# First to second expert layer: the last two units routed as one group, the exit beside the first matmul group, weight splits moved into the head's second matmuls

## The chip, the cores and the metric

The kernel runs on one core of a Trainium2 chip. The metric is the device time of one execution in microseconds; before the change the median of three runs is 629.38 us (629.02 to 632.44). Engines are TensorE (PE, with its weight loads shown as PEld), VectorE (DVE), ScalarE (ACT), GpSimd (POOL) and SyncE (SP, which here issues DMAs). Each works through its own queue in the order in which the program was written.

## What is computed

Attention over clusters, then two mixture-of-experts layers one behind the other. Both layers pick one expert of eight for each of 1536 rows of 512 numbers, multiply by two weight matrices with a ReLU between them, and scale by the gate. The second layer's routing needs the first layer's result, row by row.

```python
def _moe2_ref(x, w_gate, w_output_gate, w1, w2) -> np.ndarray:
    logits = x @ w_gate
    e_idx = np.argmax(logits, axis=1)
    ...
    eom = 1.0 / (1.0 + np.exp(-(x @ w_output_gate)))
    out = np.zeros((N, D), dtype=np.float32)
    for e in range(E):
        mask = e_idx == e
        ...
        h = np.maximum(x[mask] @ w1[e], 0.0)
        ye = h @ w2[e]
        out[mask] = gate_w[mask, None] * eom[mask, e, None] * ye
    return out.astype(np.float32)
...
    x = _moe_ref(x=x, **moe_kwargs)
    return _moe2_ref(x=x, **moe2_kwargs)
```

## The kernel before

Attention takes about the first 300 us; the change is in the two expert layers behind it. They are cut into 18 units, 0 to 8 for the first layer and 9 to 17 for the second. A unit is the rows of one expert (the largest expert of each layer is two units: 0 and 1, 9 and 10), in tiles of at most 128 rows: unit 6 has 128 and 48 rows, unit 7 128 and 40, unit 8 has 120, unit 9 two of 128, unit 10 128 and 8, unit 11 128, 128 and 16. The first unit of a layer is its head.

`run` (L1050) writes out the order of all work by hand. A unit has eight groups of first matmuls, f=0 to f=7 (`mm1`, L916: 12 matmuls each, then `hh` on ACT and the rest `hl` on DVE), and four quarters of second matmuls, d=0 to d=3 (`mm2`, L976; unit 9 takes `mm2_by_token`, L952, in which ACT copies each quarter out into `xo` and sums it into `ls`, a tile that `outs` (L936) has POOL set to zero at d=0). Ahead of each f and d, `run` takes as many steps of the open background tasks as `SB` says for a head (one for other units), and as many weight splits as the unit's row of `PIECES` says. A split is a half of one weight chunk of 1 MB: `wh` on ACT and, one split later, the rest `wl` on DVE (L820, L827); when a chunk is split its buffer is free and `pump` (L795) has SP load a next one into it (`raw`).

Background tasks are the exits. `exit1` (L1620) of a unit of the first layer is put on the list behind group `fx` of the next unit: f=7 for most, f=2 (`FB`) where the next unit is the second layer's head. Its steps: logits `pq` from the unit's result `y`, and `lt` on ACT; `pg` and the transposes `pyo` back; then `lg` on DVE, and the rows `xo` on ACT, tile by tile. The copy of the last quarter of `y` is on DVE, that of the others on ACT (L998). Units are routed in groups (`group1`): the last unit of a group goes on into `routed` (L1670): choice of the expert, counts `cs`, gate, scales `sx` and the scaling of `xo` on POOL (L1711), the places by two matmuls `ppos` (L1718, L1719), the gate's copy into the row on POOL (L1755), the write to the table `x2d` in DRAM from SP (L1760), and the inverse list by one-hot tiles `av`, `rv` and a matmul (L600). Group (4, 5) also picks the second layer's first expert and gives the list `idx2a` for unit 9. The last group has all rows in place: it gives `idx2` for the units from 10 on and issues the gathers of units 10 and 11.

A `gather` (L857) is an indirect DMA for each tile from POOL, out of `x2d` into `xg`; `meta` (L873) reads two columns of it on POOL; `entry` (L891) transposes a tile on PE (`pxt`), copies it on ACT (`xh`) and takes the rest on DVE (`xl`). For most units the entry of the next unit's tiles stands behind f=4 to f=7; in a head it stands behind d=3. A unit's gather is issued by `run` ahead of f=0 where it isn't out yet, as for unit 9, behind the steps that are due there.

In `routed`, `last` is the group with unit 8: it takes its choice at once, and has two steps of pause (`KL`) between its one-hot tiles and the inverse matmul.

Of the kernel before, what the change touches and what calls it, by code (L numbers as in the profile page):

```python
# [473 lines left out]
def turns_by(k, *chains):  # L474

    chains = list(chains)
    while chains:
        for _ in range(k):
            chains = [c for c in chains if next(c, c) is not c]
        if chains:  # L480
            yield
# [195 lines left out]
class Stage:  # L677


    def __init__(self, units, src, w1, w2, sw):  # L680
        self.src, self.w, self.sw = src, (w1, w2), sw
        self.units = [Unit(self, *u) for u in units]
        n = r = 0
        for i, u in enumerate(self.units):
            u.first, u.row = n, r
            n += len(u.tiles)
            r += u.rows
            u.closes = i + 1 == len(units) or self.units[i + 1].j != u.j
            u.opens = i == 0 or self.units[i - 1].j != u.j
        self.ranks = list(dict.fromkeys(u.j for u in self.units))  # L690
        self.E = len(self.ranks)
        self.reg = [None] * self.E
        self.exit = None


class Unit:
    def __init__(self, stage, j, tiles):
        self.stage, self.j, self.tiles, self.rows = stage, j, tiles, sum(tiles)
        self.idx = None
        self.src = stage.src  # L700
        self.gt = None
        self.by_token = False
        self.last = False
        self.xo = None


class MoE:
# [23 lines left out]
    FX = 1  # L731
    FB = 2
    FY = 7
    SA = (1, 0, 1, 0, 1, 1, 0, 1, 1, 0, 1, 1)
    SB = (1, 3, 2, 1, 1, 1, 1, 1, 1, 1, 1, 1)
    Q = 2

    def __init__(self, tc, ctx, ident, R, XW, ND, stages, ps_t):
# [237 lines left out]
    def mm2(self, u, d):  # L976
        nc = self.nc
        if u.by_token:
            return self.mm2_by_token(u, d)
        N = u.rows  # L980
        if d == 0:
            u.y = self.y.tile([128, 4, self.most], F32, tag="yt", name="yt", bufs=1)
        hh, hl = u.h
        self.need(4 * u.r + 2 + d // 2)
        wh, wl = (w.rearrange("p (a f) -> p a f", a=8) for w in self.chunk[4 * u.r + 2 + d // 2])
        p = self.ps_mm.tile([128, 512], F32, tag="m", name="py")
        s = slice(d % 2 * 128, d % 2 * 128 + 128)
        k = 0
        for (w, x) in ((wh, hh), (wl, hh), (wh, hl)):
            if u.last and k == 16:  # L990
                if d == 0:
                    self.outs(u)
                else:
                    self.turn(u, d - 1)
            for f in range(8):
                nc.tensor.matmul(p[:, :N], w[:, f, s], x[:, f, :N], start=(k == 0), stop=(k == 23))  # L996
                k += 1
        (nc.vector.tensor_copy if d == 3 else nc.scalar.copy)(u.y[:, d, :N], p[:, :N])  # L998
        if u.last and d == 3:
            self.turn(u, d)  # L1000

# [48 lines left out]
    def run(self, task):  # L1050

        units = self.units
        self.tasks.append(task)
        for i, u in enumerate(units):
            prev = units[i - 1] if i else None
            nxt = units[i + 1] if i + 1 < len(units) else None
            head = not prev or prev.stage is not u.stage
            steps = (1,) * 12 if not head else self.SB if prev else self.SA
            fx = self.FB if head else self.FX if not nxt else self.FY if nxt.stage is not u.stage else 7
            own = 4 * u.r + 8 if head else self.G  # L1060
            pieces = self.PIECES[i]
            for f in range(8):
                for _ in range(steps[f]):
                    self.step()
                if not head and self.ngather == i + 1:
                    self.gather()
                if not head and self.nmeta == i + 1 < self.ngather:
                    self.meta()
                self.pieces(pieces[f], own)
                self.mm1(u, f)  # L1070
                if f == 3 and u.closes:
                    self.limit += 1
                if prev and f == fx:
                    self.exit(prev)
                if f >= 4 and nxt and not head:
                    self.entry(nxt, f - 4)
            if u.closes:
                self.limit += 1
            for d in range(4):
                for _ in range(steps[8 + d]):  # L1080
                    self.step()
                self.pieces(pieces[8 + d], own)
                if d == 3 and u.opens:
                    self.need(4 * u.r + 3)
                    self.flags(u.r)
                self.mm2(u, d)
                if d % 2 and u.closes:
                    self.limit += 1
                if d == 1 and self.ngather == i + 2:
                    self.gather()  # L1090
                if d == 3 and self.nmeta == i + 2:
                    self.meta()
            if head:
                assert nxt.gt, "unit not gathered"
                for k in range(len(nxt.tiles)):
                    self.entry(nxt, k)
        self.exit(units[-1])
        self.step(all=True)
# [4 lines left out]
KL = 2  # L1103
# [172 lines left out]

def tile_kernel(tc, q, k, v, centroids, wg1, w11, w12, cap_in, wg2, wog2, w21, w22, out,
                prof1=(192, 304, 208, 200, 192, 176, 168, 120), prof2=(392, 272, 224, 192, 160, 128, 120, 88),
                head1=128, head2=256, cut2=5, by_token=(0, 3, 5), group1=((0, 1), (2, 3), (4, 5), (6, 7), (8,)), seq1=(1, 2, 3, 4, 5, 6, 7), seq2=(1, 6, 2, 5, 3, 4, 7), dbg=None):
    nc = tc.nc  # L1280
    P = 128
    B, NP, _, S = q.shape
# [10 lines left out]
    with ExitStack() as ctx:  # L1293
# [326 lines left out]
        def exit1(unit, ys):  # L1620

            group = of[id(unit)]
            ns, gs, u = unit.tiles, unit.gt, unit.u
# [10 lines left out]
            N = unit.rows  # L1634
# [12 lines left out]
            xo = [M.xo.tile([P, XW], F32, tag="xo", name="xo") for _ in ns]  # L1647
            xos += zip(xo, ns)
            ps = back(ys)
            yield  # L1650
            nc.gpsimd.tensor_copy(vb[:, k0:k1], unit.vb)
            nc.gpsimd.tensor_scalar(vk[:, k0:k1], unit.vb, M.okr[unit.r], None, op0=ALU.mult)
            for i, n in enumerate(ns):
# [16 lines left out]
        def routed(group, t0, T, rows):  # L1670
            lg, am, vb, vk, xos = held.pop(id(group))
            last = s1.units[-1] in group
# [19 lines left out]
            K = KC if cut else KG  # L1692
# [19 lines left out]

            if not last:
                yield from turns_by(K[1], scales())
            for _ in range(1 if last else K[5]):
                yield
            pp = M.ps_g.tile([P, 512], F32, tag="g", name="ppos2")
            nc.tensor.matmul(pp[:, :T * E], R.to[:, 0], oh2[:, t].rearrange("p a e -> p (a e)"), start=True, stop=False)  # L1718
# [1 line left out]
            if last or cut:  # L1720
                nc.tensor.matmul(pp[:, T * E:(T + 1) * E], R.to[:, 1], cs2[:, t0 + T], start=True, stop=True)
            lohi, ro = [], []
            yield

            def places():
                nc.vector.tensor_tensor(pos, pp[:, :T * E].rearrange("p (a e) -> p a e", e=E),
# [44 lines left out]
                if not last and K[4]:  # L1771
                    yield
            more = first_experts() if cut else iter(())
            for _ in range(KL if last else K[3]):
                yield
                for _ in range(2):
                    next(more, None)
# [124 lines left out]
```

## Time and profile before

| | us |
|---|---|
| median of three runs | 629.38 |
| lowest, highest | 629.02, 632.44 |
| profiled execution, its own time | 627.58 |
| its span, first to last instruction | 625.7 |
| PE busy in the span | 569.5 (91%) |
| DVE, ACT, POOL busy | 467.1, 419.9, 212.8 |

The profile is of one execution. Time in its views is counted in us from the start of the span. The passage between the layers lies between 437 (unit 8 starts), 455.5 (unit 9), 481.8 (unit 9's last matmul) and 488.5 (unit 10's first). PE's granted clock is given as a share of 2.4 GHz: 1.00 is that level, 0.50 the level of 1.2 GHz. An instruction's idle time stands in brackets behind it, with what ended it.

### The profile page before, as it was taken

To read this page: it belongs to the slowest core of one execution; us is meant where nothing else is said; L and a number is where in the kernel's file an instruction comes from. 1 tells how busy PE (TensorE), PEld (TensorE's weight loads), DVE (VectorE), ACT (ScalarE), POOL (GpSimd) and SP (SyncE) were. 2 spreads that over 40 slices of the span, in tenths; PEclk is the share of its full clock that TensorE was granted. 3 is DMA by queue.
4 is the path that set the end of the run, shared out by engine and by line. 5 is a ranking of instruction groups with operands and counts; after the bars stand their busy time and mean duration, and the time that the engine had idled before them with its cause. 6 is when DMAs were issued, how large, how long until landed. Compare 5 with 4: busy or idle time off the path is not lost.

```text
span 625.7 us, 14519 instructions
## 1 busy us (share of the span) xinstructions
PE 569.5 (91%) x5430; PEld 470.8 (75%) x5430; DVE 467.1 (75%) x1219; ACT 419.9 (67%) x885; POOL 212.8 (34%) x420
## 2 busy tenths in 40 slices
PE   6899999998999988958999998998788899999992
PEld 2766767675767666637878997997767888999992
DVE  5767777679899677756597689788776566989881
ACT  4766666776666669832676776876654466979781
POOL 8702020204150210134615268344333623253341
PEclk9899999999999999998899999999899799999998
DMA  5779391826429952314486776977754457998930
GB/s 148 212 231 275 97 216 46 210 60 151 141 89 233 252 171 82 133 56 138 130 269 204 243 244 179 304 238 244 248 181 152 164 174 238 305 308 298 321 111 20
DMA packets 75518, 117.55 MB, mean 188 GB/s; under 512 B 10504, under 2 KB 43400, under 8 KB 75441
## 3 DMA queue, kind: packets, MB, share of 16 engines
q1 hardware_dynamic: 71585, 105.96, 56.1%
q0 software_dynamic: 3264, 9.72, 4.9%
q8 instruction: 45, 0.74, 0.5%
q10 hardware_dynamic: 592, 0.87, 0.4%
q14 instruction: 32, 0.26, 0.1%
HBM read 84.28 MB, written 12.87 MB: 155 GB/s over the span
## 4 chain that ended last, share of the span: by engine, by line
PE 63%; DVE 16%; ACT 9%; DMA 5%; issue 4%; SPq 1%; POOL 0%; ACTq 0%; DVEq 0%; POOLq 0%
PE ph L930 17%; PE py L996 13%; PE av L280 9%; PE pss L238 7%; PE ppt L268 6%; DVE wl L827 3%; DVE nm L246 3%; PE pz L971 3%; ACT pe L254 2%; PE pyo L1609 2%; PE pxt L907 2%; ACT pt L270 1%; ACT wh L820 1%; DMA xg<-x2d,idx2a 1%; DMA xg<-x2d,idx 1%
## 5 line engine op out<-in xcount | busy, mean ns | idle before, releaser
L827 DVE SCALAR_TENSOR_TENSOR wl<-raw,sw,wh 128x1024 f16<-128x1024 f32 x128 | 163.5, 1283 | 18.5 <-ACT wh L820 18.4
L820 ACT ACTIVATE wh<-raw,sw 128x1024 f16<-128x1024 f32 x128 | 145.7, 1146 | 2.6 <-DMA x<-ot 2.5
L246 DVE TENSOR_REDUCE nm<-pss 128x1 f32<-128x768 f32 x96 | 91.4, 952 | 40.5 <-PE pss L238 36.8
L254 ACT ACTIVATE pe<-pss,nm 128x768 f32<-128x768 f32 x96 | 87.1, 907 | 24.2 <-DVE nm L246 24.2
L930 PEld LDWEIGHTS <-wh 128*128 128x128 f16 x1152 | 91.3, 102 | 14.2 <-issue 9.7
L238 PE MATMUL pss<-y,x 128*128 128x384 f32 x384 | 93.5, 364 | 4.1 <-ACT pe L254 3.2
L268 PE MATMUL ppt<-ident,pe 128*128 128x128 f32 x576 | 80.5, 275 | 3.3 <-ACT pt L270 1.4
L238 PEld LDWEIGHTS pss<-y,x 128*128 128x128 f32 x384 | 63.0, 190 | 24.4 <-issue 12.3
L270 ACT COPY pt<-ppt 128x384 f32<-128x384 f32 x128 | 57.9, 482 | 28.6 <-PE ppt L268 28.2
L268 PEld LDWEIGHTS ppt<-ident,pe 128*128 128x128 f32 x576 | 69.3, 142 | 8.9 <-ACT pt L270 2.3
L930 PE MATMUL ph<-xh,wh 128*128 128x192 f16 (+14 forms) x576 | 69.5, 246 | 6.7 <-DVE hl L933 5.7
L996 PEld LDWEIGHTS <-wh 128*128 128x128 f16 x960 | 72.4, 99 | 3.8 <-issue 0.5
L930 PE MATMUL ph<-xl,wh 128*128 128x192 f16 (+14 forms) x576 | 69.5, 246 | 0.2
L930 PE MATMUL ph<-xh,wl 128*128 128x192 f16 (+14 forms) x576 | 69.5, 246 | 0.0
L280 PE MATMUL av<-pt,v 128*64 128x384 f32 x384 | 68.8, 494 | 0.0
L932 ACT ACTIVATE hh<-ph 128x128 f16<-128x128 f32 (+14 forms) x144 | 44.1, 312 | 35.7 <-PE ph L930 34.3
L933 DVE SCALAR_TENSOR_TENSOR hl<-ph,hh 128x128 f16<-128x128 f32 (+14 forms) x144 | 46.4, 333 | 24.6 <-ACT hh L932 24.0
L930 PEld LDWEIGHTS <-wl 128*128 128x128 f16 x576 | 47.4, 102 | 1.9
L996 PE MATMUL py<-hl,wh 128*128 128x192 f16 (+13 forms) x480 | 46.6, 239 | 0.8 <-DVE hl L933 0.8
L996 PE MATMUL py<-hh,wh 128*128 128x192 f16 (+13 forms) x480 | 46.5, 239 | 0.6 <-DVE hl L933 0.4
L280 PEld LDWEIGHTS av<-pt,v 128*64 128x64 f32 x384 | 24.8, 136 | 28.4 <-issue 28.2
L996 PE MATMUL py<-hh,wl 128*128 128x192 f16 (+13 forms) x480 | 46.1, 239 | 0.0
(319 smaller groups left out, 858.8 us busy)
## 6 DMA issues: line engine op xcount, KB each, us to landing
raw<-in_moe_w SPq DMA_DIRECT2D x64, 1024.0 KB, 5.9
y<-kh SPq DMA_DIRECT2D x31, 192.0 KB, 4.0
x<-qh SPq DMA_DIRECT2D x30, 192.0 KB, 4.2
q<-in_q SPq DMA_DIRECT2D x8, 384.0 KB, 5.1
k<-in_k SPq DMA_DIRECT2D x8, 384.0 KB, 5.3
x<-ql SPq DMA_DIRECT2D x16, 192.0 KB, 3.6
v<-in_v SPq DMA_DIRECT2D x8, 384.0 KB, 4.1
out<-zt SPq DMA_DIRECT2D x1, 3072.0 KB, 11.0
```

The source lines that it names most:

```text
L238: nc.tensor.matmul(p[:, hf, :W], xx[:, c * P:(c + 1) * P], yy[:, hf * W:(hf + 1) * W], start=a, stop=o)
L246: nc.vector.tensor_reduce(nm, p[:, :, :W], axis=AX.XY, op=ALU.max, negate=True)
L254: nc.scalar.activation(pe, p[:, :, :W], AF.Exp, bias=d["nm", c, j], scale=1.0, accum_out=d["sm"][:, c, j:j + 1])
L268: nc.tensor.transpose(p[:, kc * P:(kc + 1) * P], pe[:, kh, kc * P:(kc + 1) * P], ident)
L270: eng(pt[:, kh * HALF:(kh + 1) * HALF, (c % HALF) * P:(c % HALF + 1) * P], p.rearrange("p (a b) -> p a b", a=HALF))
L280: nc.tensor.matmul(p[j * D:(j + 1) * D, :W], d["v"][:, j, kc, :], d["pt", hf, j][:, kc, :], start=(kc == 0), stop=(kc == C - 1))
L820: nc.scalar.activation(hi[:, :, s], x[:, :, s], AF.Copy, scale=sw)
L827: nc.vector.scalar_tensor_tensor(lo[:, :, s], x[:, :, s], sw, hi[:, :, s], op0=ALU.mult, op1=ALU.subtract, accum_out=fl)
L930: nc.tensor.matmul(p[:, :N], w[:, c, fs], x[:, c, :N], start=(k == 0), stop=(k == 11))
L932: nc.scalar.activation(hh[:, f, :N], p[:, :N], AF.Relu)
L933: nc.vector.scalar_tensor_tensor(hl[:, f, :N], p[:, :N], 0.0, hh[:, f, :N], op0=ALU.max, op1=ALU.subtract)
L996: nc.tensor.matmul(p[:, :N], w[:, f, s], x[:, f, :N], start=(k == 0), stop=(k == 23))
```

## The change

- `group1` becomes (0,1), (2,3), (4,5), (6), (7,8): unit 6 is routed alone, the last two units of the first layer as one group of three tiles.
- `FB` 2 to 0: unit 8's exit goes on the list behind f=0 of unit 9, not f=2; `SB` becomes ones. Unit 8's exit leaves out one pause (behind `pyo`), the last group has one pause more ahead of `ppos`, none behind it, and one more ahead of the inverse matmul.
- Unit 8's copy of the last quarter of `y` moves from DVE to ACT.
- `PIECES` of unit 9: splits at f=7 and d=0 to d=3, in place of f=1, f=7, d=1, d=3; unit 10 loses the one at f=0.
- Unit 10's entry: tile 0 ahead of d=2 of unit 9, tile 1 ahead of d=3, in place of both behind d=3.
- The gathers behind d=1 run one unit further ahead in the second layer.

```diff
@@ MoE @@
-              (0, 1, 0, 0, 0, 0, 0, 1, 0, 1, 0, 1),
-              (1, 0, 0, 0, 1, 0, 0, 0, 0, 1, 0, 1),
+              (0, 0, 0, 0, 0, 0, 0, 1, 1, 1, 1, 1),
+              (0, 0, 0, 0, 1, 0, 0, 0, 0, 1, 0, 1),
...
-    FB = 2
+    FB = 0
...
-    SB = (1, 3, 2, 1, 1, 1, 1, 1, 1, 1, 1, 1)
+    SB = (1, 1, 1, 1, 1, 1, 1, 1, 1, 1, 1, 1)
...
-        (nc.vector.tensor_copy if d == 3 else nc.scalar.copy)(u.y[:, d, :N], p[:, :N])
+        (nc.vector.tensor_copy if d == 3 and (u.last or not u.ends) else nc.scalar.copy)(u.y[:, d, :N], p[:, :N])
...
+                if head and prev and d >= 2:
+                    for k in range(d - 2, len(nxt.tiles), 2):
+                        self.entry(nxt, k)
                 self.mm2(u, d)
                 if d % 2 and u.closes:
                     self.limit += 1
-                if d == 1 and self.ngather == i + 2:
-                    self.gather()
+                if d == 1 and not head:
+
+                    for _ in range(i + 3 + (u.stage is not units[0].stage) - self.ngather):
+                        self.gather()
                 if d == 3 and self.nmeta == i + 2:
                     self.meta()
-            if head:
+            if head and not prev:
...
-group1=((0, 1), (2, 3), (4, 5), (6, 7), (8,))
+group1=((0, 1), (2, 3), (4, 5), (6,), (7, 8))
@@ exit1, routed @@
             ps = back(ys)
-            yield
+            if not unit.ends:
+                yield
...
-            for _ in range(1 if last else K[5]):
+            for _ in range(2 if last else K[5]):
                 yield
...
             lohi, ro = [], []
-            yield
+            if not last:
+                yield
...
-            for _ in range(KL if last else K[3]):
+            for _ in range(KL + 1 if last else K[3]):
```

(`ends` is true for the last unit of a layer, `last` for the last unit of all.)

## Rows read from the trace of the kernel before

**Rows 1.** Waits of PE from 290 to 626: total us, times, longest us.
```profile
PE pxt L907 <- DMA xg<-x2d,idx: 4.6, 1, 4.6
...
PE pxt L907 <- DMA xg<-x2d,idx2a: 2.0, 1, 2.0
PE ppos L600 <- DVE rv L595: 1.9, 1, 1.9
...
PE ppos L1719 <- DVE cs L1699: 1.0, 1, 1.0
```

**Rows 2.** Busy us by stretch: length, PE, PEld, DVE, ACT, POOL; PEclk, DMA share, GB/s.
```profile
437.34:455.52 18.18, 14.99 (x223) 13.75 (x220) 14.18 (x41) 13.35 (x27) 6.57 (x13) 0.91 0.77 261
455.52:471.28 15.76, 12.72 (x125) 10.72 (x122) 12.28 (x56) 9.02 (x23) 5.75 (x14) 1.00 0.43 143
471.28:481.80 10.52, 10.52 (x99) 9.27 (x96) 8.72 (x42) 4.32 (x10) 3.28 (x5) 1.00 0.40 127
481.80:488.45 6.65, 1.79 (x10) 1.32 (x9) 0.14 (x1) 1.32 (x5) 5.27 (x14) 0.85 0.80 281
488.45:493.30 4.85, 4.76 (x42) 4.59 (x42) 2.46 (x7) 1.85 (x4) 4.07 (x11) 0.50 0.01 3
```

**Rows 3.** Timeline of PE: start us, us, instruction, idle before and its end.
```profile
445.07 0.71 PE L907 MATMUL pxt<-ident,xg 128*128 128x128 f32 x4 [2.04 <-DMA xg<-x2d,idx2a]
...
486.54 1.64 PE L907 MATMUL pxt<-ident,xg 128*128 128x128 f32 x8 [4.59 <-DMA xg<-x2d,idx]
```

**Rows 4.** Timeline of POOL, 418 to 438: a scaling of group (4, 5), unit 9's gathers.
```profile
418.24 3.91 POOL L1711 TENSOR_SCALAR xo<-xo,sx 128x512 f32<-128x512 f32 x4 [0.82 <-DVE sx L671]
...
435.94 1.11 POOL L867 DMA_INDIRECT xg<-x2d,idx2a  x1 [2.92 <-PE py L996]
437.35 1.48 POOL L867 DMA_INDIRECT xg<-x2d,idx2a  x1 [0.30 <-PE py L996]
```

**Rows 5.** Timeline of DVE: routing steps, a rest of the split, the copy of y.
```profile
416.57 0.75 DVE L1699 TENSOR_TENSOR cs<-cs,oh 128x8 f16<-128x8 f16 x4
...
437.95 0.32 DVE L998 COPY yt<-py 128x168 f32<-128x168 f32 x1
...
472.21 0.42 DVE L933 SCALAR_TENSOR_TENSOR hl<-ph,hh 128x256 f16<-128x256 f32 x1
472.54 0.15 DVE L1726 TENSOR_TENSOR pos<-ppos,base 128x8 f32<-128x8 f32 x1
...
475.44 1.27 DVE L827 SCALAR_TENSOR_TENSOR wl<-raw,sw,wh 128x1024 f16<-128x1024 f32 x1
...
477.21 0.18 DVE L649 TENSOR_REDUCE idx<-w 128x4 int32<-128x32 f32 x1
```

**Rows 6.** Timeline of POOL, 474 to 487: scaling of group (8), first and last gather.
```profile
474.36 0.70 POOL L1711 TENSOR_SCALAR xo<-xo,sx 120x512 f32<-120x512 f32 x1
...
479.21 2.10 POOL L867 DMA_INDIRECT xg<-x2d,idx  x1 [3.99 <-DVE p2nov L663]
...
485.52 0.92 POOL L867 DMA_INDIRECT xg<-x2d,idx  x1 [0.30 <-issue]
```

**Rows 7.** Timeline of ACT: unit 8's last split, unit 9's first copy out.
```profile
457.33 1.14 ACT L820 ACTIVATE wh<-raw,sw 128x1024 f16<-128x1024 f32 x1
...
475.25 0.47 ACT L973 ACTIVATE xo<-pz,u 128x256 f32<-128x256 f32 x1 [3.31 <-POOL ls L939]
```

**Rows 8.** Chain that ended last, around unit 8's small matmuls: start us, us, work.
```profile
463.26 0.34 PE pq L1637 x8
...
463.91 1.33 PE ph L930 x12
...
466.13 3.93 PE ph L930 x36
```

**Rows 9.** DMA issues at 485.5 (gather) and 464.5 (write): KB, us to landing.
```profile
xg<-x2d,idx POOLq DMA_INDIRECT x1, 2.9
...
x2d<-xo SPq DMA_DIRECT2D x1, 262.0 KB, 2.1
```

More of the change, by code (lines that the diff above doesn't have):

```diff
@@ L689, in __init__ @@
             u.opens = i == 0 or self.units[i - 1].j != u.j
+            u.ends = i + 1 == len(units)
         self.ranks = list(dict.fromkeys(u.j for u in self.units))
@@ L703, in __init__ @@
         self.last = False
+        self.ends = False
         self.xo = None
@@ L1278, in tile_kernel @@
                 prof1=(192, 304, 208, 200, 192, 176, 168, 120), prof2=(392, 272, 224, 192, 160, 128, 120, 88),
-                head1=128, head2=256, cut2=5, by_token=(0, 3, 5), group1=((0, 1), (2, 3), (4, 5), (6, 7), (8,)), seq1=(1, 2, 3, 4, 5, 6, 7), seq2=(1, 6, 2, 5, 3, 4, 7), dbg=None):
+                head1=128, head2=256, cut2=5, by_token=(0, 3, 5), group1=((0, 1), (2, 3), (4, 5), (6,), (7, 8)), seq1=(1, 2, 3, 4, 5, 6, 7), seq2=(1, 6, 2, 5, 3, 4, 7), dbg=None):
     nc = tc.nc
```

## The prediction

> **What bounds the kernel now.** I first read the list of TensorE's waits over the two expert layers [rows 1]: it says what the end is paying for, since TensorE (PE) is busy almost everywhere else. Two lines stand out, both transposes `pxt` that wait for a gather: 4.6 us for the gather of unit 10 (tile from `idx`), 2.0 us for that of unit 9 (`idx2a`). Two smaller ones, 1.9 and 1.0 us, are routing matmuls that wait for VectorE (DVE). Then the table by stretches [rows 2], which cuts the passage into unit 8, unit 9's first matmuls (15.76 us), its second matmuls (10.52 us, no idle), the gap up to unit 10's first matmul (6.65 us) and the stretch behind it, in which the granted clock is 0.50, so the 1.2 GHz level of the two; before the gap it was 1.00 and PE had then stood for 4.6 us. That stretch is 4.85 us of work worth 2.4 at full clock. From unit 9's first matmul to a unit 10 at full clock the kernel pays 15.76 + 10.52 + 6.65 + 2.4 = 35.3 us. So up to 9 us can be won there, if nothing else comes late. The other rows say what comes late: the two waits where they stand on PE [rows 3], POOL's queue around the gathers [rows 4, 6], DVE's routing steps [rows 5], ScalarE (ACT) [rows 7], unit 8's small matmuls on PE [rows 8] and the landing of gathers and writes [rows 9]. I count from the start of unit 9's f=0 (455.52) as time 0.
>
> **Part 1: unit 6 routed alone, one unit earlier.** The group of units 6 and 7 is now unit 6 alone (2 tiles), and its routing runs inside unit 8. By the code, its step at unit 8's f=0 issues `cs`, the gate, the scales and two POOL scalings of `xo`; only then does `run` issue the gather of unit 9, and unit 9's `meta`. POOL works in order, so the gather, which started at 435.94 before [rows 4], now stands behind the scalings. They wait for `sx`. DVE gets to `cs` after the copy of unit 7's last quarter, done at 438.27 [rows 5]; from the first of four `cs` to the scaling it was 1.67 us (416.57 [rows 5] to 418.24 [rows 4]), two `cs` fewer at 0.19 leave 1.3: 439.5. A scaling is 0.98 us in the group of four [rows 4] and 0.70 alone [rows 6], so two are 1.4 to 2.0, and the gather starts at about 441.4 (441.0 to 441.6), its second tile 1.4 later (as 435.94 to 437.35) at 442.8. That is 5.4 us later than now. How long it takes to land is bounded by 2.9 us [rows 9] and 7.7 us (437.35 to the transpose at 445.07 [rows 3, 4]). I take 4.0, since the load of the next weights that shared the DMA engines at 442.6 is now held behind the new x2d write on SP's queue, which itself stands behind `meta` and the group's small POOL copies. So the second tile is there at 446.8 (445.7 to 450.5), PE can transpose it then and not at 445.07, and what follows is PE's own work as before: unit 8 ends **1.7 us later**, and a bit more, 2.0, for the extra DVE steps between (4.2 us of them in f=0 to f=7, mostly in time that DVE now has while PE waits); range +1.2 to +5.5. Weights held back on SP would be due at unit 8's d=3, some 8 us after they are freed; that covers their landing.
>
> **Part 2: unit 9's first matmuls.** Gone are the two DVE waits of the group (6, 7), 1.91 and 0.99 [rows 1], and with `SB` at ones the steps spread evenly. New: unit 8's exit now issues `pq` before f=1, and it needs the copy of unit 8's last quarter, which moves from DVE to ACT behind the split that starts at 457.33 and takes 1.04 up to its successor [rows 7]. The copy ends at about 458.7, PE is there at 456.85: a new wait of **1.9 us**. Behind the copy on ACT stands only `hh` of f=0, which PE doesn't miss. So the first matmuls take 15.76 - 2.9 + 1.9 = 14.7 us. The moved splits (row 9 of `PIECES`, five where there were four) cost nothing here: ACT and DVE idle in the second matmuls, 4.3 and 8.7 of 10.5 us busy [rows 2]. That the splits come three in a row behind each other there matters for part 3.
>
> **Part 3: the way to unit 10's gather.** Now `ppos` comes before f=5, at 10.1 (five groups of 1.33, the wait of 1.9, and 1.5 for unit 8's small matmuls, 463.26 to 466.13 less one group of 1.33 [rows 8]), and DVE starts the long step at about 10.6, behind `hl` of f=4. For one tile the scaling began 1.8 us into that step (472.54 to 474.36) and the last `rv` ended after 2.9, where the next split starts [rows 5, 6]. With three tiles I take 2.0 and 3.6. POOL then copies three gates and scales three tiles, 0.70 to 0.98 each: the last is ready at 15.0 to 16.5, and the write lands 2.1 us [rows 9] to 4.1 us (the end of its scaling at 475.06 to the gather at 479.21 [rows 6], if it was the write that the gather waited for) later, 17.2 to 20.6. On the other side the inverse matmul comes before d=0; DVE is through `rv` at 14.2 and must first do `hl` of f=5 to f=7, 0.42 each, and a split, 1.27; then `tab` and `idx`, 0.7 from the end of the split at 476.7 to 477.39 [rows 5]: 17.4. The gather starts at **18.6** (17.4 to 20.6). Its landing has 7.3 us as its own row (479.21 to the transpose at 486.54 [rows 3, 6], 4.6 of them PE's wait) and 2.9 at the other end [rows 9]; I take 6.0, nearer to its own, because a weight load is issued behind it again: 24.6.
>
> The entry of unit 10 is issued ahead of the second matmuls d=2. PE gets there at 14.7 + 5.26 = 19.95 and, in order, stands **4.6 us** before work that doesn't need the gather. So the stall isn't covered, it's moved by half of the second matmuls. Then 0.5 for the transposes, 5.26 for d=2 and d=3, 0.3 for the second tile: 30.7 at full clock. A stall of this length was followed by the lower clock before [rows 1, 2]; I put in the same 2.4: **33.1**. Against 35.3 that is a gain of 2.2.
>
> What hides under it: by the code POOL now has five gathers ahead of the `memset` of `ls` for unit 9 (before, the memset came ahead of them). ACT's first copy of the second matmuls needs it; ACT waited 3.31 us for it already, at 475.25 [rows 7]. It comes 7.2 us after the first gather starts (479.21 to 486.44 [rows 6]), at 25.8. Behind it ACT has two copies (0.66), two splits (1.04), `xh` of tile 0, a third copy and split, and `xh` of tile 1, so x is whole at about 32. Hidden by 1 us; at full clock it would be the bound.
>
> The Trainium skill ("DMA: Bandwidth & Descriptors", Anatomy of one DMA) says that DMA engines don't wait on semaphores and the wait is spent on the issuing sequencer; by that the memset is late whenever the write is. No row of this kernel shows something queued behind such a wait.
>
> **Part 4: the rest.** Gathers one unit deeper in layer 2: no wait in [rows 1] is for a later gather, so nothing is won, and POOL has the time; 0, at most 0.3 either way. Sum: +2.0 - 2.2 = **-0.2 us**. It's made in the profiled execution (span 625.7, time 627.58) and applied to the median, 629.38: **629.2**.
>
> **The rivals.**
> (a) Slower: gathers behind other transfers take 7.3 to 7.7 us in both places, as two of the rows do. Then unit 9's second tile comes at 450.5, +5.4 in unit 8; unit 10's first at 25.9, which makes 34.4, a gain of 0.9. Sum +4.5, **633.9**. For it: these very gathers took that long; against it: the weight load beside the first one is held back. Each us of landing counts twice, once in each place, so it decides from a mean landing of about 6.7 us, against the 5.0 of the forecast.
> (b) Faster: the write lands after 2.1 us and the gather after 4. It starts at 17.5, lands at 21.5, PE waits 1.5 us and the clock stays up. PE would be ready at 27.6, but ACT's chain behind the memset binds: 17.5 + 6 to 7.2 + 6 = 30. Gain 5.3, less 1.5 in unit 8: -3.8, **625.6**. For it: the DMA engines moved 127 GB/s in the second matmuls against 261 in unit 8 [rows 2]; against it: in the gap in which the 7.3 us gather landed they moved 281, a weight load issued just behind it, and that load is issued behind it again.
> The same page's fit, 2.0 us and the bytes over 436 GB/s, would make an estimated 2.6 us of the 0.27 MB gather; by it this rival would hold. The rows have 2.9 at best, 7.3 here.
> (c) The change does all it says: x arrives by d=2, no stall, no slow clock, ACT not in the way. 14.7 + 10.5 + 0.8 = 26.0, gain 9.3 - 2.0: **622.1**. Against it: gather by 17 and landing in 2.9 at once, and the memset.
>
> **How the numbers follow.** 0.5% is 3.1 us, about what a measurement of this kernel tells from no change. The forecast, 626.3 to 632.5, has 0.47; (a) 0.25; (b) 0.22; (c) 0.06. Faster 0.28, within 0.47, slower 0.25. The range leaves out (c) and the outer part of (a): 624.5 to 634.2.
>
> **What would show it.** Right: the gather of unit 9 starts about 5 us later after unit 8 begins, behind two scalings; PE waits at `pxt` of unit 9 some 4 us and at the first `pxt` of unit 10 in the middle of unit 9's second matmuls 3 to 6 us; no wait behind them; ACT's first copy of unit 9 waits for `ls` some 7 us. Wrong: no PE wait at d=2 (then b or c); the gather of unit 9 not delayed; unit 9's first matmuls longer than 15.8 us, which would be a DVE that three tiles hold up for longer than I have it.

## The result and the profile after

The change makes the kernel slower: 633.39 us (median of 20 runs) against 629.19 of the kernel before (20 runs), ratio 1.0054, interval 1.0033 to 1.0075, so about 3.4 us. The forecast was 629.2, no change. The profiled execution of after takes 633.78 with a span of 632.0.

Milestones make the traces comparable, because unit 8 starts anywhere from 437.2 to 444.4 in the spans of the traces below, whatever the kernel (attention ahead of it differs). Each length is the difference of two PE start times: the first `ph` of units 8, 9, 10 and 11, and the first `pz` of unit 9.

| us | unit 8 | unit 9, first matmuls | first `pz` to unit 10 | unit 10 | unit 8 to 11 |
|---|---|---|---|---|---|
| before, the trace of the prediction | 18.34 | 15.76 | 17.17 | 15.30 | 66.57 |
| before, second trace (e1) | 16.13 | 15.76 | 16.96 | 14.88 | 63.73 |
| before, third trace (e8) | 16.01 | 15.76 | 16.85 | 15.15 | 63.77 |
| after | 20.28 | 14.52 | 19.55 | 13.82 | 68.17 |
| after, second trace (e2) | 20.23 | 14.52 | 19.58 | 12.88 | 67.21 |

From unit 11 to the end all five take 121.6 to 122.1. So the loss is in this passage, 3.4 to 4.4 us against the second and third trace of before, and it is made in unit 8 (+4.2), won back in unit 9's first matmuls (-1.2), lost again on the way to unit 10 (+2.6) and won back in part in unit 10 (-1.1 to -2.3).

PE's waits in the expert layers of after (total us, times, longest), to be read against [rows 1]:

```profile
PE pxt L909 <- DMA xg<-x2d,idx: 6.2, 1, 6.2
PE pxt L909 <- DMA xg<-x2d,idx2a: 3.4, 1, 3.4
...
PE pq L1644 <- ACT yt L1000: 1.3, 1, 1.3
...
PE ppos L600 <- DVE rv L595: 0.5, 1, 0.5
```

Both waits for gathers are longer: 6.2 us where it was 4.6, and 3.4 where it was 2.0. The two routing waits for VectorE have shrunk (the 1.9 is now 0.5; the 1.0 at the first `ppos` is no longer among the longest), and `pq` has a new one. By stretch (unit 8, unit 9's first matmuls, d=0 and d=1, the wait, d=2 and d=3, unit 10's start; columns as in [rows 2]):

```profile
441.72:462.00 20.28, 15.60 (x229) 14.48 (x227) 16.42 (x54) 13.92 (x29) 9.12 (x21) 0.92 0.71 224
462.00:476.52 14.52, 12.63 (x123) 10.56 (x119) 9.52 (x52) 9.16 (x23) 2.72 (x8) 1.00 0.47 160
476.52:481.92 5.40, 5.40 (x48) 4.59 (x47) 5.16 (x17) 0.66 (x1) 1.94 (x2) 1.00 0.34 107
481.92:488.17 6.25, 0.00 (x1) 0.03 (x1) 1.11 (x2) 0.00 (x0) 5.07 (x4) 0.74 0.81 245
488.17:496.07 7.90, 7.90 (x56) 6.47 (x57) 3.47 (x7) 5.25 (x11) 6.93 (x21) 0.77 0.47 147
496.07:500.92 4.85, 4.72 (x75) 4.54 (x73) 0.90 (x3) 1.42 (x5) 3.55 (x4) 1.00 0.67 200
```

The fourth line is the whole wait: PE and ACT do nothing for 6.25 us in the middle of the second matmuls. Behind it d=2, d=3 and the entry take 7.90 at a mean granted clock of 0.77; unit 10 then runs at 1.00, where it ran at 0.50 before. The lower clock has moved, it isn't gone.

The timelines of after (start us, us, instruction, idle before and its end): POOL, then DVE, SP, PE and ACT around unit 10's gather.

```profile
444.01 2.32 POOL L1719 TENSOR_SCALAR xo<-xo,sx 128x512 f32<-128x512 f32 x2 [6.45 <-ACT z L552]
446.61 1.11 POOL L869 DMA_INDIRECT xg<-x2d,idx2a  x1 [0.28 <-issue]
448.03 1.01 POOL L869 DMA_INDIRECT xg<-x2d,idx2a  x1 [0.30 <-issue]
...
474.72 3.83 POOL L1719 TENSOR_SCALAR xo<-xo,sx 128x512 f32<-128x512 f32 x3
481.92 2.08 POOL L869 DMA_INDIRECT xg<-x2d,idx  x1 [3.37 <-PE pz L973]
...
489.13 0.12 POOL L941 MEMSET ls<- 128x8 f32 x1
...
476.72 1.27 DVE L829 SCALAR_TENSOR_TENSOR wl<-raw,sw,wh 128x1024 f16<-128x1024 f32 x1
...
481.75 1.28 DVE L829 SCALAR_TENSOR_TENSOR wl<-raw,sw,wh 128x1024 f16<-128x1024 f32 x1
...
475.59 3.32 SPq L1769 DMA_DIRECT2D x2d<-xo  x3
481.96 0.41 SPq L795 DMA_DIRECT2D raw<-in_moe_w  x1
...
450.22 0.66 PE L909 MATMUL pxt<-ident,xg 128*128 128x128 f32 x4 [3.40 <-DMA xg<-x2d,idx2a]
...
488.17 1.09 PE L909 MATMUL pxt<-ident,xg 128*128 128x128 f32 x4 [6.25 <-DMA xg<-x2d,idx]
...
489.29 0.47 ACT L975 ACTIVATE xo<-pz,u 128x256 f32<-128x256 f32 x1 [12.11 <-POOL u L888]
```

Both gathers stand behind work on POOL. Unit 9's stands straight behind two scalings of unit 6 (done at 446.33, the gather at 446.61). Unit 10's waits for the write of `x2d`, whose three parts SP issues as POOL finishes each row tile, at 475.59, 476.72 and 478.58. The profile puts the end of POOL's 3.37 us down to `pz` on PE, which ends at the same time; in other runs it names `wl` or `ov` on DVE. The landing of the write's last part is the steadier clue: in the ten traces of a changed kernel that have it, the gather starts 0.87 us behind it each time.

The three scalings, merged in one line of 3.83 us, take 0.84, 1.03 and 1.77 each. The last starts while DVE is in a `wl` and ends 0.6 us behind it. From 410 us on, all 31 scalings in the fourteen traces that start inside a `wl` take 1.53 to 1.77 us, and the others 0.68 to 1.03. No run moved such a `wl`, so what it costs is seen, not tested.

ACT's first copy of unit 9's results stands 12.11 us behind it all, since the zeroing of `ls` is queued behind five gathers.

### The profile page after: what moved, and what is told of

Read it like the earlier page. It is cut to its first block, busy times and chain, and to the rows that moved or that the text cites. A ratio compares the mean times of both kernels' runs of the same rounds, so it can differ in the third digit from the quotient of the medians.

```text
span 632.0 us, 14520 instructions
## 1 busy us (share of the span) xinstructions
PE 570.4 (90%) x5430; PEld 468.5 (74%) x5430; DVE 468.0 (74%) x1217; ACT 419.6 (66%) x886; POOL 215.4 (34%) x420
## 4 chain that ended last, share of the span: by engine, by line
PE 61%; DVE 17%; ACT 10%; DMA 5%; issue 4%; POOL 1%; SPq 0%; ACTq 0%; POOLq 0%; DVEq 0%
PE ph L932 16%; PE py L998 12%; PE av L280 9%; PE pss L238 7%; PE ppt L268 6%; PE pz L973 4%; DVE wl L829 3%; DVE nm L246 3%; ACT pe L254 2%; PE pyo L1616 2%; PE pxt L909 2%; ACT wh L822 2%; ACT pt L270 1%; PE plog L153 1%; DMA out<-xo,tk 1%
## 5 line engine op out<-in xcount | busy, mean ns | idle before, releaser
L932 PEld LDWEIGHTS <-wh 128*128 128x128 f16 x1152 | 88.7, 99 | 15.3 <-issue 10.8
L998 PEld LDWEIGHTS <-wh 128*128 128x128 f16 x960 | 72.4, 99 | 4.0 <-issue 0.7
L932 PE MATMUL ph<-xh,wh 128*128 128x192 f16 (+14 forms) x576 | 67.9, 241 | 7.7 <-DVE hl L935 6.8
L932 PE MATMUL ph<-xh,wl 128*128 128x192 f16 (+14 forms) x576 | 67.9, 241 | 0.1
L932 PE MATMUL ph<-xl,wh 128*128 128x192 f16 (+14 forms) x576 | 67.8, 241 | 0.2 <-issue 0.2
L932 PEld LDWEIGHTS <-wl 128*128 128x128 f16 x576 | 45.9, 99 | 2.2 <-issue 0.2
```

The source lines that it names most:

```text
L932: nc.tensor.matmul(p[:, :N], w[:, c, fs], x[:, c, :N], start=(k == 0), stop=(k == 11))
```

## The experiments

The theory after the result: (1) unit 8 pays for the gather of unit 9 behind the scalings; (2) on the way to unit 10 two bars of nearly equal height lie behind each other, the entry of unit 10 at d=2, and the zeroing of the sums behind the gathers; (3) both rest on the start of unit 10's gather, which the three scalings on POOL set through the write. The rivals: DMA landings that are slower than forecast (the prediction's rival a), or VectorE's routing of one more unit in unit 8.

**e1, e2, e8: the same kernels again.** No edit.

> The kernel before once more, for a second trace of it. Of the 6.3 us by which the two profiled executions differ, 4.5 lie ahead of unit 8 (its first matmul at 437.18 and 441.72), where both kernels issue the same instructions in the same order but for six small VectorE steps. Theory A: that is spread from one execution to the next; then this trace starts unit 8 somewhere between 435 and 443, and from there to unit 11's first matmul takes 66.6 us again (within 0.7). Rival B: the change costs something ahead of unit 8; then this trace starts unit 8 at 437 +- 1, and every trace of the changed kernel near 441.7.

> The changed kernel once more. Theory A: unit 8 starts anywhere between 435 and 443, and from there to unit 11's first matmul takes 68.2 us again (within 0.7), 1.6 more than before; the time comes out 1.6 us over the kernel before, give or take 2. Rival B: unit 8 starts at 441 to 442.5 again, and the time is 3 to 5 us over the kernel before.

> The kernel before a third time, for its trace. In the first trace unit 8 took 18.3 us with a wait of 2.0 us for unit 9's gather and the lower clock behind it, in the second 16.1 us with a wait of 1.1 us and the clock up. Theory A: the first was the rarer case, so this unit 8 takes 16 to 16.5 us, and the change costs 4 us there, not the 2 that I had from the first trace. Rival: 18.3 is the usual one.

Measured: before again 629.17 against 627.82, 1.0008 (0.9973 to 1.0043); after again 1.0052 (1.0024 to 1.008); before a third time 629.63 in one execution. Unit 8 of the kernel before, in its second trace and its third (columns as above):

```profile
441.33:457.46 16.13, 13.83 (x226) 12.80 (x224) 14.15 (x41) 13.50 (x27) 6.63 (x13) 1.00 0.86 295
```

```profile
442.05:458.06 16.01, 13.83 (x225) 12.80 (x223) 14.15 (x41) 13.51 (x27) 6.51 (x13) 1.00 0.87 294
```

Against the first line of [rows 2], the same work of some 224 matmuls took 13.83 us of PE and not 14.99, at 1.00 and not 0.91, and the wait for the second tile was half as long:

```profile
448.24 0.63 PE L907 MATMUL pxt<-ident,xg 128*128 128x128 f32 x4 [1.06 <-DMA xg<-x2d,idx2a]
```

I had expected 66.6 us from unit 8 to unit 11 in e1 and 68.2 in e2, and 63.73 and 67.21 came. So the trace on which the prediction rests had unit 8 some 2.2 us longer than the two other traces. After has 20.28 and 20.23, and the change costs 4.2 there.

**e3: unit 9's gather ahead of the steps.**

```diff
             for f in range(8):
+                if f == 0 and not head and self.ngather == i + 1:
+                    self.gather()
                 for _ in range(steps[f]):
```

> The changed kernel with one thing moved: in a unit's first group the gather that is due is issued ahead of the background steps, so that unit 9's gather no longer stands behind the two scalings of unit 6's rows on GpSimd. Theory A: the gather starts about 5 us earlier in unit 8, TensorE's wait of 3.4 us at unit 9's first transpose falls under 1.5 us (some 2 us of a wait for the second tile can stay), unit 8 takes 18.3 us in place of 20.3, and the whole time falls by 1.5 to 2 us against the changed kernel. Rival: the gather takes longer to land, because the weight load shares the DMA engines with it again, or the scalings now come later and hold back the write and the weights behind it; then unit 8 stays within 0.5 us of 20.3.

Measured: 1.0022 (0.9989 to 1.0055), where the changed kernel measured beside it had 1.0052. SP, POOL and PE of this kernel:

```profile
442.09 0.37 SPq L795 DMA_DIRECT2D raw<-in_moe_w  x1
...
440.74 1.11 POOL L869 DMA_INDIRECT xg<-x2d,idx2a  x1 [3.62 <-DVE oh L537]
442.15 1.01 POOL L869 DMA_INDIRECT xg<-x2d,idx2a  x1 [0.31 <-PE ppos L1728]
443.71 2.31 POOL L1721 TENSOR_SCALAR xo<-xo,sx 128x512 f32<-128x512 f32 x2 [0.55 <-ACT hh L934]
...
448.54 0.63 PE L909 MATMUL pxt<-ident,xg 128*128 128x128 f32 x4 [0.69 <-DMA xg<-x2d,idx2a]
```

The order on POOL is turned round, the wait of 3.4 falls to 0.7, and unit 8 takes 17.97 and not 20.28. The medians alone don't tell 1.0022 from 1.0052; the trace shows 2.3 of the 4.2 us. 1.9 are left. From the first `pz` to unit 10 this trace takes 20.40, 0.8 more than after, so unit 8 to unit 11 comes to 65.76 and not the whole 2.3 less.

**e4, e5, e6: the two bars behind unit 9.** e4 puts the entry of unit 10 back behind d=3; e5 has the zeroing ahead of the second matmuls (and so ahead of the gathers); e6 has both.

```diff
# e4
-                if head and prev and d >= 2:
-                    for k in range(d - 2, len(nxt.tiles), 2):
-                        self.entry(nxt, k)
...
-            if head and not prev:
+            if head:
# e5
-        if d == 0:
+        if d == 0 and not u.xo:
             self.outs(u)
...
+            if head and prev:
+                self.outs(u)
             for d in range(4):
```

> The changed kernel with unit 10's entry back behind the last quarter of unit 9, as before the change. Theory A: the gather lands at the same point, 26.2 us after unit 9 starts; TensorE does not wait in the middle of the second matmuls but runs on to 25.0 and waits behind them. There ScalarE sets the end, since its first copy still waits for the zeroed sums behind five gathers on GpSimd (27.3) and unit 10's xh stands behind two more copies and splits: unit 10 starts at 33.5 to 34.5 as now (34.1), but at the lower clock, so the time is 1 to 2.5 us longer than with the changed kernel. Rival: the early entry is what costs, the order of TensorE alone; then unit 10 starts by 30 and the time is 3 us or more shorter.

> The changed kernel with one thing moved: the sums of unit 9 are set to zero on GpSimd ahead of its second matmuls, so ahead of the five gathers. In the run with the late entry TensorE stood 5.4 us at its fourth quarter for ScalarE, which waits for that zeroing; with the early entry it stands 6.3 us for the gather at the third. Theory A: two bars at one place, the gather and the zeroing, each long enough alone. Then taking the zeroing away with the entry left early gives nothing: TensorE's wait at the transpose stays 6.0 to 6.5 us, unit 9's second matmuls to unit 10 stay at 19 to 19.8 us, the time within 1 us of the changed kernel, though ScalarE's wait of 12.1 us is gone. Rival: the zeroing is the bar and the gather rides with it; then the time falls by 3 us or more.

> The changed kernel with both taken away at once: sums zeroed early, and unit 10's entry behind the last quarter. Either alone changed nothing or is expected to. Theory A (two bars at one place): TensorE runs through the second matmuls without a wait, 10.5 us, waits 1 to 2 us for the gather, stays at the upper clock, and the stretch from d=0 to unit 10 takes 12.5 to 14 us in place of 19.6. The time falls by 5 to 7 us against the changed kernel, so 2 to 4 under the kernel before. Rival: a third bar (the gather lands later because a weight load gets ahead of it, ScalarE still late with xh): the stretch stays over 17 us.

Measured: e4 1.0041 (1.0011 to 1.0072), e5 1.0058 (1.0019 to 1.0097), e6 0.9996 (0.9957 to 1.0035). From the first `pz` to unit 10: 19.52, 19.29, 15.27, where after has 19.55. The lists of PE's waits from unit 8 to unit 11, in this order:

```profile
PE pz L973 <- ACT xo L975: 5.4, 1, 5.4
```

```profile
PE pxt L909 <- DMA xg<-x2d,idx: 6.4, 1, 6.4
```

```profile
PE pxt L909 <- DMA xg<-x2d,idx: 3.2, 2, 2.0
```

This is what two equal bars look like: taking away either one wins nothing, since PE runs on to the other. Without the early entry PE stands 5.4 us at the fourth quarter, because ACT, held by the zeroing, hasn't emptied the PSUM buffer of the first. With the zeroing early and the entry early it stands 6.4 at `pxt`. With neither, 4.3 us of the passage are won, and the time of the kernel before is reached, but no more: unit 8 still takes 20.29. For e4 I had expected 1 to 2.5 us more than the changed kernel, which its ratio doesn't show, and for e6 2 to 4 us under the kernel before: two waits for the gather, 1.2 and 2.0 us, were left at `pxt`.

**e7: e3 and e6 in one kernel.**

> As the run with zeroing early and entry late, and unit 9's gather ahead of the steps as well. Theory A: the parts add, for unit 8 goes from 20.2 to 18.0 us as with that move alone: 1.5 to 2 us less than without it, 7 to 9 less than the changed kernel, 4 to 6 under the kernel before. Rival: they don't add, as the weights held back behind the write of unit 6's rows come late.

Measured: 627.94, 0.9992 (0.9952 to 1.0033). Unit 8 takes 17.96, the way to unit 10 15.19, so the parts add; unit 8 to unit 11 takes 63.02 (e6 64.26), as much as the 63.7 of before. I had expected 4 to 6 us under the kernel before; 0.5 came, and the interval includes 1. PE's clock in unit 10 is 0.83, and unit 10 takes 15.35. POOL, SP (with the time that the write's last part takes to land) and PE around unit 10's gather:

```profile
467.91 3.83 POOL L1720 TENSOR_SCALAR xo<-xo,sx 128x512 f32<-128x512 f32 x3
...
475.10 2.10 POOL L869 DMA_INDIRECT xg<-x2d,idx  x1 [3.20 <-DVE wl L829]
...
468.78 3.32 SPq L1770 DMA_DIRECT2D x2d<-xo  x3
x2d<-xo SPq DMA_DIRECT2D x1, 245.6 KB, 2.5
475.15 0.41 SPq L795 DMA_DIRECT2D raw<-in_moe_w  x1
...
481.40 0.63 PE L909 MATMUL pxt<-ident,xg 128*128 128x128 f32 x4 [1.05 <-DMA xg<-x2d,idx]
484.07 0.56 PE L909 MATMUL pxt<-ident,xg 8*128 8x8 f32 x4 [2.04 <-DMA xg<-x2d,idx]
```

The gather starts 19.9 us after unit 9's f=0 (455.19) in this kernel, and just so in after and e2 to e6. `idx` is done at 472.1. The last part of the write is issued at 471.8, and by the list of DMA issues it takes 2.5 us to land; the gather follows 0.87 later. That points at the scalings.

**e9, e11: two of the three scalings on ACT.** e9 is e7 with this edit; e11 is the changed kernel with this edit alone. (4096 is `XSUM`.)

```diff
+                if last:
+                    sxx = small("sxx", T)
+                    nc.vector.tensor_scalar(sxx, sx, XSUM, None, op0=ALU.mult)
                 for i, (x, n) in enumerate(xos):
-                    nc.gpsimd.tensor_scalar(x[:n, :DM], x[:n, :DM], sx[:n, i:i + 1], XSUM, ...)
+                    if last and i:
+                        nc.scalar.activation(x[:n, :DM], x[:n, :DM], AF.Copy, scale=sxx[:n, i:i + 1])
+                    else:
+                        nc.gpsimd.tensor_scalar(x[:n, :DM], x[:n, :DM], sx[:n, i:i + 1], XSUM, ...)
```

> The three edits together, and beyond them two of the last group's three row scalings on ScalarE (DVE first makes the scale times 4096), one left on GpSimd. Theory: what still holds the gather of unit 10 at 19.9 us after unit 9's f=0 is the write of x2d, which stands behind three scalings of 1.28 us in a row on GpSimd (3.83). With one on GpSimd beside two of some 0.7 on ScalarE the write is issued about 2.5 us earlier and the gather starts at 17.0 to 17.5, by when idx is there (16.8); 6.0 to 6.4 us later it lands at about 23.5, before the end of d=3 at 25. The waits at pxt of unit 10 (1.1 and 2.0) fall to under 0.5 together, unit 10's first matmul comes at about 26.5 and not at 29.7, and TensorE's granted clock stays at 1.00 in unit 10 (13 us for it, not 14.2 to 15.3). Unit 8 to unit 11: about 58 us against 63 to 64.3 of the two kernels with the three edits or without the change; the time about 0.992 of before (0.989 to 0.995). Rival 1: the gather waits for VectorE's list or for GpSimd's queue, not for the write: it stays at 19.9 and the time at 0.998 to 1.001. Rival 2: it starts earlier but lands no sooner, because the weight loads shift with it: waits of 2 to 3 us stay, 0.997.

> The changed kernel with only the two scalings moved to ScalarE: unit 9's gather still behind the steps, unit 10's entry still at d=2 and d=3, the zeroing still behind five gathers. Theory: the gather of unit 10 starts about 2.7 us earlier (17.2), lands at 23.3, TensorE waits 3.4 us at d=2 and not 6.25; unit 10 starts at about 31 and not 34.1; unit 8 stays at 20.2. That wins 3 us: the time of the kernel before, 1.000 (0.997 to 1.003). Rival: the zeroing of the sums behind the gathers then binds, TensorE waits in the fourth quarter for a PSUM buffer that ScalarE hasn't emptied, and under 1.5 us are won: 1.003.

Measured: e9 623.24 against 629.38 of the kernel before, 0.9904 (0.9869 to 0.994); e11 627.32, 0.9964 (0.9934 to 0.9994). POOL, ACT, SP and PE of e9:

```profile
472.07 0.84 POOL L1726 TENSOR_SCALAR xo<-xo,sx 128x512 f32<-128x512 f32 x1
...
477.65 1.11 POOL L869 DMA_INDIRECT xg<-x2d,idx  x1 [4.58 <-DVE ov L660]
...
471.78 1.33 ACT L1724 ACTIVATE xo<-xo,sxx 40x512 f32<-40x512 f32 x2 [2.29 <-DVE sxx L1721]
...
472.94 1.23 SPq L1776 DMA_DIRECT2D x2d<-xo  x3
x2d<-xo SPq DMA_DIRECT2D x1, 245.6 KB, 3.0
479.39 0.41 SPq L795 DMA_DIRECT2D raw<-in_moe_w  x1
...
484.73 0.94 PE L909 MATMUL pxt<-ident,xg 128*128 128x128 f32 x8
```

3.83 us of scalings have become 0.84 beside 1.33, the write is out by 474.17, and the gather starts at 18.3 (unit 9's f=0 is at 459.36), 1.6 earlier; I had expected 17.0 to 17.5, but the write, issued at once in three parts, takes 3.0 to land and not 2.5. The gather again follows 0.87 later. It is enough: `pxt` has no wait any more, the granted clock stays at 1.00, unit 10 takes 13.38, and unit 8 to unit 11 takes 58.10, 5.6 less than before. In e11 the same start shows at 18.3 (unit 9's f=0 at 463.07):

```profile
481.36 1.10 POOL L869 DMA_INDIRECT xg<-x2d,idx  x1 [4.73 <-DVE ov L660]
...
483.10 0.41 SPq L795 DMA_DIRECT2D raw<-in_moe_w  x1
...
484.95 0.63 PE L909 MATMUL pxt<-ident,xg 128*128 128x128 f32 x4 [1.57 <-DMA xg<-x2d,idx]
```

e11 does better than the 1.000 expected. The wait falls from 6.25 to 1.57, more than the 1.6 us that the gather starts earlier; the landing itself takes 3.6 here and not 6.25 (below). First `pz` to unit 10 takes 15.40, where after has 19.55. Of this, 1.75 is a wait of unit 10's first `ph` for `xh` on ACT, which still waits 8.09 for the zeroing: the second bar is lower, not gone. So one engine's 3.83 us, on no list of PE's waits, set the height of both bars.

**e10, e12: what is left in units 8 and 9.** e10 is e9 with the last copy of unit 8 back on VectorE; e12 is e10 with one weight split moved from unit 8's f=1 to unit 9's f=3.

```diff
# e10
-(nc.vector.tensor_copy if d == 3 and (u.last or not u.ends) else nc.scalar.copy)
+(nc.vector.tensor_copy if d == 3 else nc.scalar.copy)
# e12, rows 8 and 9 of PIECES
-              (0, 1, 0, 1, 1, 0, 0, 1, 1, 1, 1, 1),
-              (0, 0, 0, 0, 0, 0, 0, 1, 1, 1, 1, 1),
+              (0, 0, 0, 1, 1, 0, 0, 1, 1, 1, 1, 1),
+              (0, 0, 0, 1, 0, 0, 0, 1, 1, 1, 1, 1),
```

> As the run with the scalings on ScalarE, and the copy of unit 8's last quarter of y back on VectorE. Theory: pq waits 1.33 us for that copy on ScalarE, which stands behind a split of 1.14; on VectorE it stands behind the split's other half, which is done about 1.7 us after unit 9's f=0, when TensorE gets to pq. The wait falls to 0.3 or less, unit 9's first matmuls take 13.3 to 13.6 us and not 14.5, and everything behind moves with it: 1.0 us, ratio 0.990 against 0.992. Rival: the time comes back as a wait at ppos for VectorE, whose routing steps start no earlier (they hang on the rows that ScalarE makes): 14.3 to 14.5, no difference.

> As the run with the copy back on VectorE, and one weight split of unit 8 (ahead of f=1) moved to unit 9 (ahead of f=3). Theory: the 1.9 us that unit 8 is still longer than before the change (17.96 against 16.0 to 16.1) are VectorE's time: routing of unit 6 adds 2.1 us to it there (16.25 busy of 17.97 against 14.15 of 16.0), and TensorE waits for hl. One split of 1.27 less: unit 8 takes 16.7 to 17.2, unit 9's first matmuls no more than 0.3 longer, since VectorE has idle time there; ratio about 0.989 against 0.990. Rival: TensorE's small waits in unit 8 hang on the order of the steps, not on VectorE's sum; unit 8 stays at 17.9, and the split in unit 9 delays the routing, so that the time is the same or 0.5 to 1 us longer.

Measured: e10 622.99, 0.9887 (0.9843 to 0.9932); e12 622.04, 0.9881 (0.9842 to 0.9921). In e10 the wait at `pq` is 0.21 and not 1.33, unit 9's first matmuls take 13.70 and not 14.53, unit 8 to unit 11 57.28. The medians don't tell e9, e10 and e12 apart; the 0.8 us of e10 are seen in the trace only. Unit 8 in e10 and in e12:

```profile
441.90:459.87 17.97, 14.70 (x229) 13.07 (x227) 16.25 (x54) 13.89 (x29) 9.92 (x21) 1.00 0.79 252
```

```profile
441.83:459.72 17.89, 15.36 (x230) 14.07 (x228) 15.11 (x52) 12.79 (x28) 7.98 (x21) 0.90 0.78 247
...
449.23 0.63 PE L909 MATMUL pxt<-ident,xg 128*128 128x128 f32 x4 [1.99 <-DMA xg<-x2d,idx2a]
```

In e10 VectorE is busy 16.25 of 17.97 us and PE waits 2.0 for `hl` in four places (1.1 in two in e1's trace of before). In e12 it is busy 15.11 and none of these waits is left, so they were VectorE's. But PE now reaches the second `pxt` earlier, stands 1.99 us for the gather, the clock falls to 0.90, and unit 8 is as long as ever. So unit 8 has two bars again, VectorE's routing of unit 6 and the landing of the second tile. Which edit would take both away wasn't tried, and how much of the 1.9 us is VectorE's stays open: PE's idle time in unit 8 is 1.0 us longer in e10 than in e1, its busy time 0.9.

e10 beats both kernels: 1.1% under the one before, whose ratio stands above, and by the two ratios (0.9887 over 1.0054) 1.7% under the changed one. e12 adds nothing that can be measured. Its trace is of the slowest of its six executions: there unit 10's second tile also lands late, PE stands 1.70 for it, and unit 8 to unit 11 takes 59.89. I had expected unit 8 at 16.7 to 17.2 in e12. Of the rivals named above, VectorE's routing is seen in the waits for `hl`, and a landing slower than forecast doesn't hold for unit 8 of the changed kernel, where it was 3.6.

## Why the prediction was wrong

**Part 1, the price in unit 8: right of after, wrong of before.** The prediction adds 2.0 us to the unit 8 of its one trace, which makes 18.34 + 2.0 = 20.34; it took 20.28 and 20.23. The scalings start 2.3 after unit 8 as forecast, take 2.32 (forecast 1.4 to 2.0), and the gather lands after 3.6 (4.0). What failed is the term it's set against: the sum is made in that trace and applied to the median, and its 18.34 (18.18 in [rows 2], which begins 0.16 late) holds the granted clock of 0.91 and, in [rows 3], the wait of 2.04. Two more traces have 16.13 and 16.01 with waits of 1.06 and 0.94. So "+2.0" was +4.2. That is the mis-sized term, 2.2 us of the 3.6 between the forecast and the measurement. The clock of 0.91 in the row was a hint, no more: in the kernel before it came in one of three traces, while the changed unit 8 has 0.92 and 20.2 to 20.4 us in all six traces with its gather behind the scalings (after, e2, e4, e5, e6, e11). Only a second trace could tell.

Three readings in this part are wrong without deciding it. The landing of 4.0 came close, but not for the reason given. The load at 442.62 was issued 5.3 us behind the second tile's gather; a nearer one, at 437.99, was issued 0.6 behind it. In after the same load (442.52) goes 4.1 ahead of the gather. In e3 it stands beside the second tile's gather again (442.09 and 442.15), the tile is transposed 6.4 later, and that although the load that was named is held back to 451.63. The 2.9 of [rows 9] is of unit 11's last tile of 16 rows, not of 128. And 445.7 against 445.07 gives +0.6 as the low end, or +0.9 with the extra DVE steps, not +1.2.

**Part 2, unit 9's first matmuls: right.** 14.7 forecast, 14.52 measured. The new wait at `pq` is 1.33 (forecast 1.9), and 0.5 of the old wait at the inverse matmul stayed.

**Part 3, the way to unit 10: right in kind, 1.0 us short.** PE does stand in the middle of the second matmuls, at d=2, before work that doesn't need the gather, 6.25 us (forecast 4.6; 1.3 of the 1.65 more is the gather's later start). The gather starts at 19.9 and not at 18.6; it's inside the range of 17.4 to 20.6. The term: the scalings take 3.83 together, and not three times 0.70 to 0.98, the values of [rows 4, 6], 2.1 to 2.9. The 0.98 was a mean of four, of which one started beside a `wl` and took 1.55 and the others 0.69 to 0.75; here the third stands beside a `wl` and takes 1.77. The landing, 6.25, is near the 6.0 taken. Unit 10 starts 34.07 after unit 9's f=0 (34.10 in e2), at full clock; forecast 33.1. Before it was 35.3 in the first trace, and 34.7 to 34.9 in the other two by the same sum (15.76 + 16.96 + 14.88 - 12.88, the last being unit 10 of e2 at full clock). So the gain of 2.2 was 0.6 to 0.8. That is the second mis-sized term, 1.4 to 1.6 us: 1.0 in the way to unit 10 and the rest again in the base. With the first it makes the 3.6 between forecast and measurement in full: 4.2 - 0.7 = 3.5, and 3.4 were measured.

**The cover named for the zeroing** was right in the sum, and its reason was incomplete. The zeroing ends 7.3 us after the first gather starts (forecast 7.2); ACT's wait for it is 12.11, where the forecast has some 7, and in after nothing was lost by it. But the prediction followed only ACT's chain up to unit 10's entry and overlooked that PE's fourth quarter needs the PSUM buffer of the first. e4 shows it: as soon as the entry isn't early, PE stands 5.4 for it.

**The rivals.** (a), 633.9, is close to the time but isn't what happened: it has landings of 7.3 to 7.7 in both places, and they were 3.6 and 6.25, mean 4.9, where the forecast has 5.0. (b) and (c) need the gather earlier, and in after it came later. e9 comes near (c), with four edits that the change doesn't have: gather at 18.3, no stall, clock at 1.00; first `pz` to unit 10 takes 12.22, against the 11.3 of (c) (26.0 less 14.7).

The Trainium skill ("DMA: Bandwidth & Descriptors", Anatomy of one DMA) has the wait for a DMA's input spent on the sequencer that issues it. The trace agrees: POOL stands 3.37 us before the gather at 481.92, with the zeroing queued behind it, and ACT stands 12.11. By the fit on that page of the Trainium skill the gather was an estimated 2.6 us; for 128 rows the traces have 3.4 at best, and 6.25 here.

**What would have shown it** was named rightly: the gather behind two scalings, PE's wait at `pxt` of unit 9 (3.4, forecast some 4) and at the first `pxt` of unit 10 in the middle of the second matmuls (6.25, forecast 3 to 6), no wait behind them. ACT's wait for `ls` was 12.1, forecast some 7, and the gather of unit 9 starts 6.1 later after unit 8 begins, forecast about 5. In kind all steps came as forecast; the base of unit 8 and the gain of part 3 were the wrong sizes, and they decided the sign.

## What to carry to other kernels

Before a stretch of one trace is used as the base of a sum, look at its granted clock and at a second trace: here one stretch of 18 us differed by 2.2 between executions of the same kernel, in a change that costs 3.4. When a stalled engine's wait is moved, list everything that it needs behind the new place, PSUM buffers too; two bars of one height show no gain when either is taken away alone, and both may hang on one cause further up. That cause was an engine off PE's list of waits: ask what starts the transfer that is waited for, and shorten that, instead of ordering the work around the wait. And before a mean of a merged line is used as a price, look at its longest instruction and at what ran beside it.

## What the runs showed of the hardware

A gather of 128 rows landed 3.6 us after its start on POOL when the last weight load had been issued 4.1 us before it, or the next one followed 1.7 us later (unit 9 in after, 446.61 to 450.22; unit 10 in e11, 481.36 to 484.95 with the load at 483.10). It landed 6.25 to 6.4 later when a load of 1 MB was issued within 0.1 us of it (after, 481.92 and 481.96; e5, 6.41; e7, 475.10 and 475.15 to 481.40), and 6.5 in e12, where the second tile's gather starts at 442.70 and a load at 442.63. The traces of before (first, e1, e8) bound this: with the load 1.1 to 1.2 us behind (479.21 and 480.37) unit 10's gather still took 6.9 to 7.3. Its time on POOL was 2.1 in most of the slow landings, where it starts inside a `wl` on VectorE (481.75 in after), and 0.9 to 1.2 with no `wl` beside it; but it was 1.0 in e12's slow one, so that alone doesn't make the difference. No run moved the load alone, nor such a `wl`, so the link is seen, not proven.

The granted clock was 0.90 to 0.92 in each unit 8 in which PE had stood 1.99 us or more at a `pxt` (2.04 before, 1.99 in e12, 3.2 to 3.4 in after, e2, e4, e5, e6 and e11), and 1.00 in those with 1.06 or less (e1, e8, e3, e7, e9, e10). In two unit 8s a wait of 2 us came with its own length and 0.7 to 1.2 us more PE time for the same matmuls (15.36 in e12 against 14.70 in e10, 14.99 in before against 13.83 in e1). The length of a wait alone doesn't tell: behind 1.70 us at a `pxt` unit 10 of e12 has 0.88, behind 1.75 at its first `ph` unit 10 of e11 has 1.00.
